# Schedule prices changed, data work taken off GpSimd, and 13 weight pieces of the second MoE converted early and kept in DRAM

## The chip, the cores and the metric

The kernel runs on one core of a Trainium2 chip. Its engines each run their own queue of instructions in order: TensorE (PE, matmuls), VectorE (DVE), ScalarE (ACT), GpSimd (POOL) and SyncE (SP, which here only issues DMAs). The metric is the device time of one execution in microseconds (us), the median of several runs.

## The reference

Three stages follow each other. The weights `w1`, `w2`, `w3`, `w_out` and `w_in` arrive as 64-bit floats, all else as 32-bit.

```python
# attention: 4 batches, 8 heads, 576 tokens, head size 64, mask by blocks of 64
scores = where(block_i >= block_j, scale * q @ k.T, -1e9)
x = softmax(scores) @ v                                  # -> (2304, 512)
# first MoE, d_ff 768
h = maximum(maximum(x @ w1, x @ w2), x @ w3);  y = h @ w_out
# second MoE, d_ff 2048
h = y @ w_in;  g = h * cos(h);  out = g @ w_out          # -> (2304, 512)
```

## The kernel before

**Split products.** Each 32-bit operand is split into a rounded part `hi` and a rest `lo`, and a product is three matmuls (hi·hi, hi·lo, lo·hi). Splitting takes a copy (`R.copy`) and a subtraction (`R.sub`).

**Weights.** `convert` (line 419) makes 32-bit values of a 64-bit piece of 128x512 and splits it: a DMA of 512 KB into `raw`, a scaling of the low words in place (`raw<-raw`) and of the high words (`t<-raw`), three DVE steps on `t` (shift `t<-t`, merge `t<-raw,t`, and the add, which the trace calls CUSTOM_DVE_ANT_0 and the order ISA), the copy to `hi`, the subtraction to `lo`. There are 24 pieces for the first MoE (`whi`/`wlo`, `vhi`/`vlo`) and 32 for the second: 16 of `w_in` and 16 of `w_out`.

**Attention.** There are 32 items, one for a batch, a half of the queries and a pair of heads. An item runs: scores `S` on PE, maxima (`stat<-S`) on DVE, exponentials into `prob` on ACT with sums into `stat`, reciprocal on DVE, scaling of the rows of `prob` (`scale_rows`, line 234, 4 or 5 instructions), transposes `tb`, evacuation to `pt`, product with `v` into `X`, evacuation to `x`, then `xhi` and `xlo`. There is one `prob` buffer, so the next item's exponentials wait for this item's transposes. The first 8 items (`NATIVE`) do not split their operands.

**First MoE as filler.** Whenever 4 items have finished a half of a batch, 22 units of the first MoE (matmuls into `psm` from `xhi`, `xlo`) are queued and PE takes them between attention steps. Their results need the pool `wk`, which opens only once item 7 has used its operands (line 733). Results `y` go to DRAM.

**Second MoE.** The 2304 tokens are five chunks: four of 512 and one of 256. For each of 16 feature pieces `fc` there are 12 matmuls of `hstage` (`psm<-yh`, ...), element work (`th`, `gh`, `gl`), and 12 of `ostage` (`po`). Weight pieces are converted while chunk 0 runs: 7 of `w_in` ahead of it, and in it one of `w_out` for each `fc` and one of `w_in` for every second (lines 849 to 854). Their pool `wc` takes the space of the first MoE's weights and opens when its last matmul is done.

**What sets the order.** All operations are recorded first. `Plan.run` (line 276) then plays them through a list schedule with a price for each (`price`, line 243), emits every engine's instructions in that order, and for those that may run on several engines (`choose`: copies, scalings, subtractions) takes the engine that finishes first by price, with the price multiplied by `WEIGHT` (line 134). So a price moves both the order and the choice of engine. All emitted instructions have line L208 in the trace.

Of the kernel before, what the change touches and what calls it, by code (L numbers as in the profile page):

```python
# [8 lines left out]
F32 = mybir.dt.float32  # L9
F32R = mybir.dt.float32r  # L10
# [4 lines left out]
ALU = mybir.AluOpType  # L15
# [4 lines left out]
P = 128  # L20
# [4 lines left out]
def f32(ap):  # L25
    return ap.bitcast(F32)
# [104 lines left out]
class Plan:  # L131
    CROSS = 35.0
    COLD = 30000.0
    WEIGHT = {"DVE": 2.5, "ACT": 1.0, "POOL": 2.0}

    def __init__(self, tc):
        self.tc, nc = tc, tc.nc
# [105 lines left out]
    def price(self, engine, method, outs, ins, kw):  # L243


        if engine == "SP":
            tiles = outs + ins
            return 600.0, 2000.0 + sum(v.n * v.rows * 4 for v in tiles[:1]) / 240.0, False
        n = outs[0].n
        if engine == "PE":  # L250
            late = 190.0
            if method == "transpose":
                return 109.0, late, False
            dt = ins[0].buf.dt
            if dt == F32:
                return 4 * n / 2.4 + 13, late, False
            load = ins[0].n / 1.2
            return (max(n / 2.4 + 3, 65.0) if dt == BF16 else max(n / 2.4 + 13.5, load)), late, False
        psum = any(v.buf.psum for v in outs + ins)
        if method == "tensor_reduce":  # L260
            n = ins[0].n
        if engine == "ACT":
            scaled = isinstance(kw.get("scale"), View)
            return (n * 0.833 + (55 if psum else 100) + 95 * ("bias" in kw) + 95 * scaled
                    + 93 * ("accum_out" in kw)), 112.0, False
        if engine == "DVE":
            sb = [v for v in ins if not v.buf.psum]
            fast = method in ("tensor_copy", "tensor_scalar", "memset") and not psum
            two = method in ("tensor_tensor", "scalar_tensor_tensor") and len(sb) > 1
            if method == "reciprocal":  # L270
                return 70.0 + 5 * n, 100.0, False
            return n * (0.52 if fast else 1.04) + 68, 88.0, fast or two
        return (n * 2.35 + 75 if method == "tensor_tensor" else n * 1.04 + 90), 45.0, method != "memset"


    def run(self):
# [102 lines left out]
def fused_kernel(tc, qk, v2, w1, w2, w3, wout, w_in2, w_out2, out):  # L379
# [3 lines left out]
    NFF = w1.shape[0]  # L383
    NFC = w_in2.shape[0]
    DM = wout.shape[2]
    NK = DM // P
# [4 lines left out]
    R = Plan(tc)  # L391
    const = R.open(name="const", bufs=1)
    cv = R.open(name="cv", bufs=1)
# [3 lines left out]
    dram = R.open(name="dram", bufs=1, space=DRAM)  # L397
# [48 lines left out]
    for u in range(2):  # L446
        f = Half()
# [130 lines left out]
    def pv(it):  # L578
        f = it.f
        n = f.n  # L580
        h, l = xhi[it.half][:, it.pair], xlo[it.half][:, it.pair]
        where = {}
        for c, (j, b) in enumerate(f.order):
            where.setdefault(j, []).append((c, b))
        if it.native:
            X = ps_x.tile([P, 512], F32, "X", tag="X", bufs=2)
        else:
            x32 = at.tile([P, NLOW], F32, "x32", tag="x32")
        for e in range(2):
            a, o = 64 * e, 64 - 64 * e  # L590
            if not it.native:
                X = ps_x.tile([P, 512], F32, "X", tag="X", bufs=2)
            for j in range(f.nj):
                c0, b0 = where[j][0]
                nb = len(where[j])
                q0 = 64 * (b0 - f.first)
                if not it.native and q0 >= f.both:

                    v = it.vs[:, j, 2 * e:2 * e + 2].rearrange("p a d -> p (a d)")
                    dst = X[:, f.both:2 * n - f.both].then(  # L600
                        lambda ap, q=q0 - f.both: ap.rearrange("p (c q) -> p c q", c=2)[:, :, q:])
                    dst.n = 2 * (n - q0)
                    R.tensor.matmul(dst, v, it.pt[:, :, c0:c0 + nb, a:a + 64], start=j == 0, stop=j == f.nj - 1,
                                    skip_group_check=True)
                    continue
                with R.unit():
                    for i in range(1 if it.native else 2):
                        p = it.pt[:, i, c0:c0 + nb, a:a + 64]
                        if it.native:
                            R.tensor.matmul(X[a:a + 64, q0:n], it.vr[:, j, e], p, start=j == 0,  # L610
                                            stop=j == f.nj - 1, skip_group_check=True)
                        else:
                            v = it.vs[:, j, 2 * e:2 * e + 2].rearrange("p a d -> p (a d)")
                            R.tensor.matmul(X[:, q0:n], v, p, start=j == 0 and i == 0, stop=j == f.nj - 1 and i == 1,
                                            skip_group_check=True)
            if not it.native:
                R.scalar.copy(x32[a:a + 64, :n], X[o:o + 64, :n])
                R.vector.tensor_tensor(x32[a:a + 64, :n], X[a:a + 64, :n], x32[a:a + 64, :n], ALU.add)
                R.vector.tensor_tensor(x32[a:a + 64, f.both:n], X[a:a + 64, n:2 * n - f.both], x32[a:a + 64, f.both:n],
                                       ALU.add)  # L620
        if it.native:
            R.copy(h, X[:, :n])
            R.vector.tensor_tensor(l, X[:, :n], f32(h), ALU.subtract)
        else:
            R.copy(h, x32[:, :n])
            R.sub(l, x32[:, :n], f32(h))
# [49 lines left out]
        return units + [lambda d=d: ygroup(d) for d in range(NK)]  # L676


    def conv_w(n, pool, bufs):
        if n < 3 * NFF:  # L680
            j, m = divmod(n, 3)
            convert((w1, w2, w3)[m][j], whi[j][:, m].rearrange("p k e -> p (k e)"),
                    wlo[j][:, m].rearrange("p k e -> p (k e)"), pool, bufs)
        else:
            j = n - 3 * NFF
            convert(wout[:, j], vhi[:, j], vlo[:, j], pool, bufs)

    NI = len(items)
    LA = 2
    fill, owed, converted = [], [0.0], [0]  # L690
# [3 lines left out]
    def conv_next():  # L694
        n = converted[0]
        if n < 4 * NFF:
            if n % 3 < 2 and not wk:
                conv_w(n, cv_start, 4)
            else:
                conv_w(n, cv, 2)  # L700
            converted[0] += 1

    def units(share):
# [14 lines left out]
    for n in range(NI + 1):  # L718
        conv = CONV.get(n, (0, 0, 0))
        if n:  # L720
            transposes(items[n - 1])
        for step in range(3):
            if step == 1 and n < NI:
                scores(items[n])
                if n + LA < NI:
                    load(items[n + LA])
            if step == 2 and n:
                it = items[n - 1]
                pv(it)
                if it.pair == HP - 1:  # L730
                    if it.n == HP - 1:
                        R.close(cv_start)
                        wk = R.open(cv_start, name="wk", bufs=1)
                    fill += zip([*range(1, 3 * NFF + 1)] + NK * [4 * NFF], moe1_units(it.b, it.half))
            for _ in range(conv[step]):
                conv_next()
            units((0.3, 0.35, 0.35)[step])
        if n + 1 < NI:
            prep(items[n + 1])
    R.close(ps_x)  # L740
    R.close(at)


    chunks = [(t, min(CH, NT - t)) for t in range(0, NT, CH)]
    NA = 7
    wb = R.open(at, name="wb", bufs=1, side="right")
    ps_o = R.open(ps_x, name="ps_o", bufs=1, space=PSUM, side="right")
    ps_h = R.open(ps_x, name="ps_h", bufs=1, space=PSUM, side="right")
# [1 line left out]
    wih, wil, woh, wol = {}, {}, {}, {}  # L750
    raw_from = [0]

    def conv_in(fc, pool):
        raw_from[0] += 1
        wih[fc] = pool.tile([P, NK, P], F32R, f"wih{fc}")
        wil[fc] = pool.tile([P, NK, P], F32R, f"wil{fc}")
        convert(w_in2[fc], wih[fc].rearrange("p k e -> p (k e)"), wil[fc].rearrange("p k e -> p (k e)"),
                (cv, wb)[raw_from[0] % 2], 2)

    def conv_out(fc, pool):  # L760
        raw_from[0] += 1
        woh[fc] = pool.tile([P, DM], F32R, f"woh{fc}")
        wol[fc] = pool.tile([P, DM], F32R, f"wol{fc}")
        convert(w_out2[:, fc], woh[fc], wol[fc], (cv, wb)[raw_from[0] % 2], 2)

    yh, yl = {}, {}

# [37 lines left out]
    def hstage(c, fc):  # L805
        n = chunks[c][1]
        ps = bank()[:, :n]
        prods = [(wih[fc], yh[c]), (wih[fc], yl[c]), (wil[fc], yh[c])]
        for k in range(NK):
            with R.unit():  # L810
                for i, (w, x) in enumerate(prods):
                    R.tensor.matmul(ps, w[:, k], x[:, k, :n], start=(k == 0 and i == 0),
                                    stop=(k == NK - 1 and i == 2))
        t = wk2.tile([P, CH], F32, "th", tag="t", bufs=3)[:, :n]
        gh = wk2.tile([P, CH], F32R, "gh", tag="gh", bufs=3)[:, :n]
# [30 lines left out]
    for n in range(len(seq) + LAG):  # L846
        if n < len(seq):
            c, fc = seq[n]
# [62 lines left out]
```

## Time and profile before

| | us |
|---|---|
| median of 3 runs | 966.83 (965.18 to 967.91) |
| the profiled execution, own time | 967.8 |
| its span, first to last instruction | 966.0 |
| PE busy | 911.8 (94%) |
| DVE busy | 642.9 (67%) |
| ACT busy | 465.4 (48%) |
| POOL busy | 135.4 (14%) |

The profile calls matmul ends modelled, so PE's busy share alone does not say that it runs at its peak; counts of matmuls in a stretch (the x numbers) say more. The program has these stretches: the 8 unsplit items with PE waiting often (to about 94 us), attention with first-MoE filler (to about 520), the last of the first MoE (to about 555), chunk 0 with the weight conversions (to about 645), the other chunks (to the end).

### The profile page before, as it was taken

To read this page: it belongs to the slowest core of one execution; us is meant where nothing else is said; L and a number is where in the kernel's file an instruction comes from. 1 tells how busy PE (TensorE), PEld (TensorE's weight loads), DVE (VectorE), ACT (ScalarE), POOL (GpSimd) and SP (SyncE) were. 2 spreads that over 40 slices of the span, in tenths; PEclk is the share of its full clock that TensorE was granted. 3 is DMA by queue.
4 is the path that set the end of the run, shared out by engine and by line. 5 is a ranking of instruction groups with operands and counts; after the bars stand their busy time and mean duration, and the time that the engine had idled before them with its cause. 6 is when DMAs were issued, how large, how long until landed. Compare 5 with 4: busy or idle time off the path is not lost.

```text
span 966.0 us, 14289 instructions
## 1 busy us (share of the span) xinstructions
PE 911.8 (94%) x5356; PEld 800.2 (83%) x5356; DVE 642.9 (67%) x1286; ACT 465.4 (48%) x1035; POOL 135.4 (14%) x168
## 2 busy tenths in 40 slices
PE   4878999999999999999999999899999999999998
PEld 3645989899998998998999988668888888888897
DVE  5887966677567576576665979996555544555554
ACT  5656455565556565555663566654224222322233
POOL 2322121011111011101011245520000000000000
PEclk9998999999999999999999999999999999999999
DMA  5454441211122111212003534532001000100010
GB/s 166 156 163 153 135 136 50 74 56 36 37 62 63 55 36 43 61 40 85 15 1 105 165 108 148 157 110 88 0 1 50 16 1 1 44 1 1 1 44 23
DMA packets 35749, 64.89 MB, mean 67 GB/s; under 512 B 9312, under 2 KB 20576, under 8 KB 35680
## 3 DMA queue, kind: packets, MB, share of 16 engines
q1 hardware_dynamic: 35680, 63.98, 21.3%
q8 instruction: 42, 0.69, 0.3%
q14 instruction: 27, 0.22, 0.1%
HBM read 54.53 MB, written 9.44 MB: 66 GB/s over the span
## 4 chain that ended last, share of the span: by engine, by line
PE 65%; DVE 17%; ACT 10%; issue 5%; POOL 2%; DMA 1%; ACTq 0%; SPq 0%; DVEq 0%; POOLq 0%
PE psm L208 35%; PE po L208 17%; PE S L208 7%; ACT prob L208 5%; DVE t L208 5%; DVE stat L208 5%; PE tb L208 4%; PE X L208 2%; DVE th L208 1%; DVE hm L208 1%; DVE pt L208 1%; POOL prob L208 1%; ACT hh L208 1%; DVE x L208 1%; DVE vs L208 1%
## 5 line engine op out<-in xcount | busy, mean ns | idle before, releaser
L208 PE MATMUL psm<-xhi,whi 128*128 128x320 f32 (+1 forms) x576 | 176.8, 307 | 4.7 <-DVE hm L208 3.4
L208 PE MATMUL psm<-xlo,whi 128*128 128x320 f32 (+1 forms) x576 | 170.6, 296 | 0.9 <-DVE xlo L208 0.9
L208 PE MATMUL psm<-xhi,wlo 128*128 128x320 f32 (+1 forms) x576 | 170.4, 296 | 0.0
L208 ACT ACTIVATE th<-th,halfpi 128x512 f32<-128x512 f32 (+1 forms) x80 | 54.4, 681 | 162.4 <-DVE th L208 162.4
L208 PE MATMUL psm<-yh,wih 128*128 128x512 f32 (+1 forms) x320 | 119.6, 374 | 5.7 <-ACT wih L208 5.7
L208 DVE TENSOR_REDUCE stat<-S 128x1 f32<-128x320 f32 (+8 forms) x144 | 64.4, 485 | 86.4 <-PE S L208 75.7
L208 PE MATMUL psm<-yh,wil 128*128 128x512 f32 (+1 forms) x320 | 119.6, 374 | 0.7 <-DVE wil L208 0.7
L208 PE MATMUL psm<-yl,wih 128*128 128x512 f32 (+1 forms) x320 | 119.2, 372 | 0.0
L208 PEld LDWEIGHTS psm<-xhi,whi 128*128 128x128 f32 x576 | 109.4, 190 | 6.4 <-DVE hm L208 4.5
L208 PE MATMUL po<-wol,gh 128*128 128x512 f32 x288 | 112.8, 392 | 0.0
L208 PE MATMUL po<-woh,gh 128*128 128x512 f32 x288 | 112.6, 391 | 0.0
L208 PE MATMUL po<-woh,gl 128*128 128x512 f32 x288 | 112.4, 390 | 0.0
L208 POOL TENSOR_SCALAR prob<-prob,stat 128x64 f32<-128x64 f32 (+8 forms) x100 | 63.2, 647 | 351.1 <-DVE stat L208 273.0
L208 PEld LDWEIGHTS psm<-xlo,whi 128*128 128x128 f32 x576 | 109.4, 190 | 1.2 <-DVE xlo L208 1.1
L208 PEld LDWEIGHTS psm<-xhi,wlo 128*128 128x128 f32 x576 | 109.1, 189 | 0.0
L208 ACT ACTIVATE prob<-S,stat 128x128 f32<-128x128 f32 (+8 forms) x144 | 74.7, 528 | 62.6 <-DVE stat L208 62.1
L208 DVE TENSOR_SCALAR th<-psm 128x512 int32<-128x512 f32 (+1 forms) x80 | 50.7, 635 | 57.7 <-PE psm L208 52.1
L208 DVE TENSOR_TENSOR th<-psm,th 128x512 f32<-128x512 f32 (+1 forms) x80 | 50.9, 636 | 51.0 <-ACT th L208 51.0
L208 PE MATMUL tb<-ident,prob 128*128 128x128 f32 x400 | 64.9, 286 | 13.9 <-DVE pt L208 6.6
L208 PEld LDWEIGHTS psm<-yh,wih 128*128 128x128 f32 x320 | 60.6, 189 | 17.9 <-ACT wih L208 6.6
L208 DVE TENSOR_TENSOR gl<-th,gh 128x512 fp32r<-128x512 f32 (+1 forms) x72 | 46.6, 647 | 42.4 <-ACT gh L208 42.2
L208 PEld LDWEIGHTS psm<-yh,wil 128*128 128x128 f32 x320 | 60.6, 189 | 12.9 <-DVE wil L208 1.9
(99 smaller groups left out, 1805.9 us busy)
## 6 DMA issues: line engine op xcount, KB each, us to landing
raw<-w SPq DMA_DIRECT2D x18, 512.0 KB, 3.8
raw<-w_in SPq DMA_DIRECT2D x16, 512.0 KB, 3.4
raw<-w_out SPq DMA_DIRECT2D x16, 512.0 KB, 3.7
vr<-v SPq DMA_DIRECT2D x16, 320.0 KB, 3.2
qk<-qk SPq DMA_DIRECT2D x12, 416.0 KB, 3.2
out<-osb SPq DMA_DIRECT2D x18, 256.0 KB, 2.0
qk<-qk SPq DMA_DIRECT2D x12, 320.0 KB, 3.0
vr<-v SPq DMA_DIRECT2D x16, 192.0 KB, 2.5
```

What stands on the lines that cost most here:

```text
L208: return lambda: getattr(real, method)(*[value(a) for a in args], **{k: value(a) for k, a in kw.items()})
```

## The change

Three things change. (1) `WEIGHT` of POOL goes from 2 to 100, so the schedule never chooses POOL: its 159 data instructions move to DVE and ACT (DVE goes from 1288 to 1419 instructions, ACT from 893 to 921, PE stays at 5250). (2) Prices change: POOL's, outputs with gaps (+120 ns on ACT and DVE), and the two additions that read `X` across partitions (+118 ns). (3) While items after number 9 run, `ahead()` converts 13 pieces of the second MoE (9 of `w_in`, 4 of `w_out`) into a buffer `both` and stores it to DRAM as `kept`; chunk 0 loads these with one DMA each. The remaining 19 pieces are converted as before. `hi` and `lo` of a piece now share one tile, which the order names `w_in` or `w_out`.

```diff
-    WEIGHT = {"DVE": 2.5, "ACT": 1.0, "POOL": 2.0}
+    WEIGHT = {"DVE": 2.5, "ACT": 1.0, "POOL": 100.0}
...
+        spread = 120.0 * (outs[0].hi - outs[0].lo + 1 > n)
...
-        return (n * 2.35 + 75 if method == "tensor_tensor" else n * 1.04 + 90), 45.0, method != "memset"
+        return (n * 3.3 + 75 if method == "tensor_tensor" else max(400.0, n * 1.04 + 195)), 45.0, method != "memset"
...
-                R.vector.tensor_tensor(x32[a:a + 64, :n], X[a:a + 64, :n], x32[a:a + 64, :n], ALU.add)
+                R.vector.tensor_tensor(x32[a:a + 64, :n], X[a:a + 64, :n], x32[a:a + 64, :n], ALU.add).cost += 118.0
...
+    NA = 7
+    AHEAD = [("in", fc) for fc in range(NA, NFC)] + [("out", fc) for fc in range(3, NFC - 1, 3)]
+    kept = {}
+
+    def ahead():
+        if len(kept) < len(AHEAD) and converted[0] == 4 * NFF:
+            kind, fc = AHEAD[len(kept)]
+            both = cv.tile([P, 2, 512], F32R, "both", tag="raw", bufs=CVR)
+            convert(w_in2[fc] if kind == "in" else w_out2[:, fc], both[:, 0], both[:, 1], cv, CVR)
+            kept[kind, fc] = dram.tile([P, 2, 512], F32, f"kept_{kind}{fc}")
+            R.sync.dma_start(kept[kind, fc], f32(both))
...
+        if n > 9 and n % 3:
+            ahead()
...
+    def conv(kind, fc, pool, src):
+        w = pool.tile([P, 2, 512], F32R, f"w_{kind}{fc}")
+        if (kind, fc) in kept:
+            R.sync.dma_start(f32(w), kept[kind, fc])
+        else:
+            raw_from[0] += 1
+            convert(src, w[:, 0], w[:, 1], (cv, wb)[raw_from[0] % 2], 2)
+        return w
```

The scaling of the first item of the second half of batch 0 (item 4) stands like this on POOL before:

```order
L208 TENSOR_SCALAR prob<-prob,stat_162 128x384
L208 TENSOR_SCALAR prob<-prob,stat_162 128x448
L208 TENSOR_SCALAR prob<-prob,stat_162 128x512
L208 TENSOR_SCALAR prob<-prob,stat_162 128x576
L208 TENSOR_SCALAR prob<-prob,stat_253 128x384
```

and like this on DVE now, where the reciprocal is followed by two of the four at once:

```order
L208 TENSOR_SCALAR stat_169<-stat_169 128x4
L208 ISA t<-raw,t 128x1024
L208 RECIPROCAL stat_169<-stat_169 128x4
L208 TENSOR_SCALAR prob<-prob,stat_169 128x512
L208 TENSOR_SCALAR prob<-prob,stat_169 128x576
L208 TENSOR_TENSOR wlo_466<-t,whi_445 128x512
```

The other two (384 and 448) stand on ACT now. POOL has no row of `prob` left.

In the attention stage, DVE around the first split item's output (`x`, then `xlo`) reads before:

```order
L208 TENSOR_TENSOR x_1498<-X,x_1498 64x320
L208 TENSOR_TENSOR vs<-vr,vs 128x3x128
L208 TENSOR_TENSOR x_1498<-X,x_1498 64x192
L208 TENSOR_TENSOR x_1498<-X,x_1498 64x320
L208 TENSOR_TENSOR x_1498<-X,x_1498 64x192
L208 CAST xhi_234<-x_1498 128x320
L208 TENSOR_TENSOR pt<-tb,pt 128x512
L208 TENSOR_TENSOR xlo_239<-x_1498,xhi_234 128x320
```

and now, with one early conversion (`t`, then `both`) and the start of the next behind `xlo`:

```order
L208 TENSOR_TENSOR x_1356<-X,x_1356 64x192 x2
L208 TENSOR_SCALAR t<-t 128x512
L208 TENSOR_TENSOR xlo_248<-x_1356,xhi_245 128x320
L208 SCALAR_TENSOR_TENSOR t<-raw,t 128x512
L208 ISA t<-raw,t 128x1024
L208 TENSOR_TENSOR both<-t,both 128x512
L208 TENSOR_TENSOR hm<-psm,hm 128x256 x2
L208 TENSOR_TENSOR hl<-hm,hh 128x256
L208 TENSOR_TENSOR hm<-psm,hm 128x256
L208 TENSOR_SCALAR t<-t 128x512
```

The evacuations of the filler (`hm`) now have conversion steps ahead of them.

On SP, at the end of the first MoE (its last stores are `y_1_...`), the queue before alternates loads of both weights:

```order
L208 DMA y_1_6209<-hm 128x256 x2
L208 DMA raw<-w_in 128x1024
L208 DMA y_1_6209<-hm 128x256 x2
L208 DMA raw<-w_out 128x1024 x2
L208 DMA raw<-w_in 128x1024
L208 DMA raw<-w_out 128x1024 x2
L208 DMA raw<-w_in 128x1024
```

and now it loads `w_out` and then all 13 kept pieces in a row, of which the first rows are:

```order
L208 DMA raw<-w_out 128x1024 x2
L208 DMA y_1_6308<-hm 128x256
L208 DMA raw<-w_out 128x1024
L208 DMA w_in_6436<-kept_in_1452 128x1024
L208 DMA w_in_6443<-kept_in_1565 128x1024
L208 DMA w_out_6451<-kept_out_3178 128x1024
L208 DMA w_in_6460<-kept_in_1830 128x1024
```

After chunk 0's first `th` DVE had 21 of the ISA steps before, and has 8 now.

## Rows read from the trace of the kernel before

**Rows 1.** Windows: busy us (count) by engine, clock, DMA share, GB/s.
```profile
0.00:94.00 94.00, 66.68 (x306) 44.09 (x307) 68.97 (x175) 55.56 (x137) 24.86 (x41) 0.93 0.51 157
130.00:260.00 130.00, 124.00 (x895) 117.63 (x895) 86.70 (x197) 72.95 (x190) 18.82 (x28) 1.00 0.21 63
260.00:388.00 128.00, 122.75 (x887) 117.23 (x887) 85.22 (x194) 72.75 (x190) 17.57 (x29) 1.00 0.18 52
388.00:516.00 128.00, 122.69 (x885) 117.36 (x884) 83.77 (x192) 71.95 (x188) 15.48 (x27) 1.00 0.13 40
516.00:560.00 44.00, 44.00 (x338) 42.78 (x337) 34.14 (x64) 22.58 (x44) 8.34 (x10) 1.00 0.53 175
560.00:600.00 40.00, 40.00 (x176) 32.62 (x175) 38.31 (x59) 26.79 (x45) 19.25 (x15) 1.00 0.33 100
600.00:650.00 50.00, 43.57 (x179) 33.94 (x178) 47.49 (x73) 29.66 (x51) 24.31 (x12) 0.97 0.44 137
650.00:700.00 50.00, 50.00 (x220) 40.91 (x218) 29.67 (x45) 17.73 (x29) 0.00 (x0) 1.00 0.15 48
```

**Rows 2.** Waits of PE between 590 and 660 us: total, times, longest.
```profile
PE psm L208 <- ACT wih L208: 5.7, 2, 4.2
```

**Rows 3.** Chain that ended last, 0 to 105 us: start, us, what.
```profile
41.52 2.49 POOL prob L208 x5
...
66.55 0.14 POOL prob L208
66.69 0.93 issue
67.62 2.19 POOL prob L208 x3
...
93.73 7.24 PE psm L208 x48
```

**Rows 4.** Waits of PE weight loads, 100 to 530 us.
```profile
PEld tb L208 <- DVE pt L208: 11.1, 21, 1.1
```

**Rows 5.** Groups by form on DVE, 560 to 650 us: busy us, mean ns.
```profile
L208 DVE CUSTOM_DVE_ANT_0 t<-raw,t 128x1024 uint16<-128x1024 uint16 x21 | 17.5, 848 | 0.0
L208 DVE SCALAR_TENSOR_TENSOR t<-raw,t 128x512 int32<-128x512 int32 x21 | 17.3, 838 | 0.0
L208 DVE TENSOR_SCALAR t<-t 128x512 int32<-128x512 int32 x21 | 12.2, 593 | 0.4 <-ACT t L208 0.4
L208 DVE TENSOR_TENSOR gl<-th,gh 128x512 fp32r<-128x512 f32 x6 | 5.2, 869 | 0.6 <-ACT gh L208 0.6
```

**Rows 6.** The same view, 130 to 516 us.
```profile
L208 DVE TENSOR_TENSOR hl<-hm,hh 128x320 fp32r<-128x320 f32 x16 | 7.9, 492 | 6.4 <-ACT hh L208 6.3
...
L208 DVE CUSTOM_DVE_ANT_0 t<-raw,t 128x1024 uint16<-128x1024 uint16 x2 | 1.4, 692 | 0.1
L208 DVE SCALAR_TENSOR_TENSOR t<-raw,t 128x512 int32<-128x512 int32 x2 | 1.4, 680 | 0.0
...
L208 DVE TENSOR_TENSOR vlo<-t,vhi 128x512 fp32r<-128x512 f32 x1 | 0.7, 695 | 0.0
...
L208 DVE TENSOR_SCALAR prob<-prob,stat 128x576 f32<-128x576 f32 x1 | 0.5, 512 | 0.0
...
L208 DVE TENSOR_SCALAR t<-t 128x512 int32<-128x512 int32 x1 | 0.4, 414 | 0.0
```

**Rows 7.** Groups by form on POOL, 560 to 650 us.
```profile
L208 POOL TENSOR_TENSOR wol<-t,woh 128x512 fp32r<-128x512 f32 x9 | 16.3, 1828 | 19.6 <-ACT woh L208 19.6
L208 POOL TENSOR_TENSOR gl<-th,gh 128x512 fp32r<-128x512 f32 x8 | 14.6, 1834 | 20.4 <-issue 14.5 <-ACT gh L208 5.7
```

**Rows 8.** DMA issues: KB each, median us from issue to landing.
```profile
raw<-w_in SPq DMA_DIRECT2D x16, 512.0 KB, 3.4
```

**Rows 9.** Chain that ended last, 530 to 660 us.
```profile
558.86 1.75 DMA y<-hm
```

**Rows 10.** Groups by form on ACT, whole span.
```profile
L208 ACT ACTIVATE prob<-prob,stat 128x384 f32<-128x384 f32 x11 | 6.8, 617 | 0.8 <-DVE stat L208 0.6
```

More of the change, by code (lines that the diff above doesn't have):

```diff
@@ L261, in price @@
             n = ins[0].n
+        spread = 120.0 * (outs[0].hi - outs[0].lo + 1 > n)
         if engine == "ACT":
             scaled = isinstance(kw.get("scale"), View)
-            return (n * 0.833 + (55 if psum else 100) + 95 * ("bias" in kw) + 95 * scaled
+            return (n * 0.833 + spread + (55 if psum else 100) + 95 * ("bias" in kw) + 95 * scaled
                     + 93 * ("accum_out" in kw)), 112.0, False
@@ L271, in price @@
                 return 70.0 + 5 * n, 100.0, False
-            return n * (0.52 if fast else 1.04) + 68, 88.0, fast or two
-        return (n * 2.35 + 75 if method == "tensor_tensor" else n * 1.04 + 90), 45.0, method != "memset"
+            return n * (0.52 if fast else 1.04) + 68 + spread, 88.0, fast or two
+        return (n * 3.3 + 75 if method == "tensor_tensor" else max(400.0, n * 1.04 + 195)), 45.0, method != "memset"
     def run(self):
@@ L617, in pv @@
                 R.scalar.copy(x32[a:a + 64, :n], X[o:o + 64, :n])
-                R.vector.tensor_tensor(x32[a:a + 64, :n], X[a:a + 64, :n], x32[a:a + 64, :n], ALU.add)
+                R.vector.tensor_tensor(x32[a:a + 64, :n], X[a:a + 64, :n], x32[a:a + 64, :n], ALU.add).cost += 118.0
                 R.vector.tensor_tensor(x32[a:a + 64, f.both:n], X[a:a + 64, n:2 * n - f.both], x32[a:a + 64, f.both:n],
-                                       ALU.add)
+                                       ALU.add).cost += 118.0
         if it.native:
@@ L676, in moe1_units @@
         return units + [lambda d=d: ygroup(d) for d in range(NK)]
+    CVR = 2
     def conv_w(n, pool, bufs):
@@ L699, in conv_next @@
             else:
-                conv_w(n, cv, 2)
+                conv_w(n, cv, CVR)
             converted[0] += 1
@@ L744, in fused_kernel @@
     chunks = [(t, min(CH, NT - t)) for t in range(0, NT, CH)]
-    NA = 7
     wb = R.open(at, name="wb", bufs=1, side="right")
@@ L751, in fused_kernel @@
     raw_from = [0]
-    def conv_in(fc, pool):
[L754 to L758, printed above, removed]
+    def conv(kind, fc, pool, src):
[6 more added lines that the diff above has]
+        return w
+    def conv_in(fc, pool):
+        w = conv("in", fc, pool, w_in2[fc])
+        wih[fc], wil[fc] = ([w[:, i, k * P:(k + 1) * P] for k in range(NK)] for i in range(2))
     def conv_out(fc, pool):
[L761 to L764, printed above, removed]
+        w = conv("out", fc, pool, w_out2[:, fc])
+        woh[fc], wol[fc] = w[:, 0], w[:, 1]
     yh, yl = {}, {}
@@ L811, in hstage @@
                 for i, (w, x) in enumerate(prods):
-                    R.tensor.matmul(ps, w[:, k], x[:, k, :n], start=(k == 0 and i == 0),
+                    R.tensor.matmul(ps, w[k], x[:, k, :n], start=(k == 0 and i == 0),
                                     stop=(k == NK - 1 and i == 2))
```

## The prediction

> **What bounds the kernel now.** I read the table by stretches first [rows 1], because the share of PE over the whole span (94%) hides three different states; then the waits of PE where the conversions run [rows 2], the chain in the first stretch [rows 3], and the waits of PE's weight loads in attention [rows 4].
>
> In the dense part, 650 to 700 us, PE issues 220 matmuls in 50 us, one each 0.227 us [rows 1]. That is the yardstick for chunk 0: 560 to 600 us has 176, and 176 x 0.227 = 40.0 us, so PE is full there although DVE is busy 38.3 of 40. From 600 to 650 us there are 179, so 41 are missing, 41 x 0.227 = 9.3 us. DVE is busy 47.5 of 50 there and the largest wait of PE is for a converted piece (`wih`), 5.7 us in 2 times [rows 2]. So conversions bound only these 50 us, and all that moving them can give back is about 9 us.
>
> Two more places hold idle PE. In the first 94 us PE is busy 66.7, idle 27.3; DVE is busy 69.0 and ACT 55.6 of the 94, so no engine is full: the chain steps from engine to engine, with POOL's scaling of `prob` as a link, until the filler starts at 93.7 us [rows 3]. From 130 to 516 us PE is idle 6.0 + 5.3 + 5.3 = 16.6 of 386 us, with DVE busy 255.7 (66%) [rows 1]; the largest wait there is that of transposes for `pt`, 11.1 us in 21 times, 0.53 us each [rows 4]. Elsewhere PE is full. Its number of matmuls does not change, so the change can act only through these idle times: 27 at the start, 17 in attention, 9 in chunk 0.
>
> **Chunk 0, fewer conversions.** DVE is busy 38.3 + 47.5 = 85.8 us of the 90 from 560 to 650 [rows 1]. Its conversions there fall from 21 to 8. One costs 0.848 + 0.838 + 0.593 = 2.28 us in this stretch [rows 5]; successive DVE instructions overlap by about 0.08 us each (my estimate: the durations of rows 5 and 6 against the busy time), so 13 of them take away about 28 us. Beside GpSimd the same three steps cost 2.28, where POOL is seldom busy 0.692 + 0.680 + 0.414 = 1.79 [rows 6]: 0.49 x 8 = 4 us less on the remaining 8. Against that DVE takes back what POOL did: 8 `gl` and 3 `yl` at 0.695, which is what the subtraction of that size costs without POOL's company [rows 6], 8 us. The 9 `wol` and 3 `wil` of POOL belong to pieces of which 13 have gone, so they add nothing net. DVE comes to 85.8 - 28 - 4 + 8 = about 62 of 90 us. From 516 to 560 us DVE is at 78% and PE has no idle time [rows 1], so PE becomes the bound and the 9.3 us come back; I take 9, with 5 as the lower end for waits that show up where DVE is late by an order the schedule did not foresee.
>
> The Trainium skill speaks against taking work off GpSimd here: its page "Perfetto Trace Analysis", section "Optimizing Scalar/DVE Operations", says that with DVE saturated, offloading even to GpSimd may make sense, and adds that the two share a read port, so that it might not help. By its first half alone, POOL's 23 subtractions of this stretch at 0.695 would put DVE at 101.8 of 90 us and cost 12 us. The trace goes with its second half: POOL needs 1.83 us for what DVE does in 0.695 [rows 6, 7], and DVE's own steps are longer beside it. With 13 conversions gone the first half has no hold.
>
> **The kept pieces.** The loads replace conversions with one DMA of 512 KB. A load of this size lands in 3.4 us [rows 8]; 13 in a row on SP, if none overlapped, take 44 us. They stand behind the last `y` stores, and those land at about 560.6 us [rows 9], so the last piece is there by 605. The first is wanted by the H step of `fc` 7, some 144 matmuls after PE begins chunk 0 at about 555 us: 555 + 144 x 0.227 = 588; the last at the 16th H step, past 625. So the loads lie beside matmuls with 20 us to spare; without that cover the price would be up to 3.4 us a piece. The stores during attention cost one SP entry each. Behind a store that waits for its subtraction stand loads of `qk` and `vr`; these run two items ahead, and 8 items take 130 us, so 16 us an item cover the wait. I cost both at 0.
>
> **The first 94 us, scaling without POOL.** The four POOL scalings of an item of the second half take 0.14 + 0.93 + 2.19 = 3.3 us of the chain; the five of one of the first half 2.5 [rows 3]. Now they are shared. ACT needs 0.62 for 384 columns [rows 10], DVE 0.51 for 576 [rows 6]. Of the seven items whose scaling lies before 93.7 us, two have two on each engine (about 1.3 us, gain 2.0 each), one has all four on ACT (about 2.5, gain 0.8), and four of the first half are mixed or all on DVE (about 1.2, gain 1.3 each): 4.0 + 0.8 + 5.2 = 10 us. Against it DVE gets 16 more scalings of 0.25 to 0.51 us (some 6 us) and two subtractions (1.4), so it rises from 69 to about 74 us of what would be 84 to 90, and part of these stand ahead of a maximum or a reciprocal that the chain waits for. I take 6, nearest the middle, because I cannot tell from the order which of them do. Ends: 11 gained (all of it, and the conversions a little shorter), 3 lost (all of DVE's 7 us on the chain and only 4 of the 10 gained).
>
> **Attention, more work on DVE.** From 130 to 516 us DVE gets: 13 conversions at 0.414 + 0.680 + 0.692 + 0.695 = 2.48 us [rows 6], 32 us; some 48 scalings at about 0.39 us, 19; 17 subtractions that POOL did at about 0.47, 8; together 59, so 255.7 + 59 = 315 of 386 us (82%). Eight of the conversions fall in the first of the three stretches: 86.7 + 8 x 2.48 + 8.5 = 115 of 130, 88%. Cover: PE has filler queued, and lost nothing at 78% (516 to 560 us) or at 96% (560 to 600 us) [rows 1]. For a gain speaks that POOL's steps, which were late against their prices, are gone, and that the additions of `X` and the outputs with gaps are now priced nearer to their times. I take 0, ends 6 gained and 10 lost.
>
> **The sum.** 9 + 6 + 0 = 15 us. The profiled execution took 967.8 us (span 966.0 plus 1.8), so 952.8; the median of the runs lies 1.0 lower, so 952.
>
> **Rivals.**
> - Only chunk 0 gains: the start stays at 94 us since DVE's extra steps take what POOL's scaling gave. For it: DVE is at 73% there already; against it: 3.3 us of an item were on POOL alone. 966.8 - 9 = 958.
> - All three gain by their upper ends: 11 + 6 + 9 = 26, so 941. For it: contention with POOL ends everywhere; against it: DVE at 88%.
> - The kept loads arrive late, or PE waits for something else in chunk 0, and the start gives nothing: the time stays at 966 to 967. Against it: the 20 us of cover.
> - DVE becomes the bound in attention and the kernel is slower. Place: items 9 to 23, where the conversions stand ahead of `hm` and `pt`. Price: 16 items with four groups of transposes, each waiting 0.53 us as the 21 do now [rows 4], are 34 us, against about 11 us idle there now: 23 lost, less the 15: 975. It decides from about 1 us more of PE wait for each of the 16 items. For it: 88% in the first stretch, where PE runs in a fixed order; against it: 96% in 560 to 600 us, where PE lost nothing.
>
> **How the numbers follow.** The forecast (945 to 955) 0.45; only chunk 0 (955 to 963) 0.22; all gain (937 to 945) 0.15; no change 0.06; slower by DVE 0.12. A measurement here tells 0.3% (2.9 us) from no change. Faster by more than that: 0.45 + 0.15 and nearly all of 0.22, 0.80; within it 0.06 and the rest, 0.08; slower 0.12. The range leaves out the slower rival and the lower part of the best case: 941 to 966; the likeliest case alone has 945 to 955.
>
> **What would show it.** Chunk 0: some 220 matmuls in every 50 us from the end of the first MoE, no wait of PE for a weight, DVE near 70%; a wait for a kept load would prove the third rival. Start: the filler's long run of `psm` begins at about 88 us and not at 94; at 94 or later the first rival holds. Attention: idle PE near 17 us; transposes waiting for `pt`, or filler waiting for `hm`, by 30 us or more would be the last rival. DVE's steps of a conversion at 1.8 us in all stretches would show that the longer ones were due to POOL; if they stay at 2.28, that part is wrong.

## The result, and the profile after

| | median us (lowest to highest) | profiled execution | its span |
|---|---|---|---|
| before | 966.00 (964.74 to 967.91) | 967.80 | 966.0 |
| changed | 955.46 (955.11 to 955.84) | 955.45 | 953.7 |

The ratio is 0.9882, 95% interval 0.9868 to 0.9895: 10.5 us less by the medians, 12.3 us by the two profiled spans. The forecast was 952.

The stretches of the changed kernel, in the columns of [rows 1] and in the same stretches but the last:

```profile
0.00:94.00 94.00, 70.06 (x343) 50.51 (x344) 74.12 (x204) 62.35 (x157) 1.88 (x9) 0.91 0.52 163
130.00:260.00 130.00, 124.57 (x899) 119.02 (x900) 106.52 (x245) 85.54 (x209) 0.00 (x0) 1.00 0.35 117
260.00:388.00 128.00, 123.39 (x887) 117.43 (x886) 105.17 (x247) 85.09 (x210) 0.00 (x0) 1.00 0.33 106
388.00:516.00 128.00, 122.83 (x885) 117.53 (x884) 86.14 (x203) 75.26 (x195) 0.00 (x0) 1.00 0.13 41
516.00:560.00 44.00, 44.00 (x332) 42.38 (x331) 37.57 (x79) 24.26 (x48) 0.00 (x0) 1.00 0.62 201
560.00:600.00 40.00, 40.00 (x175) 32.31 (x174) 35.88 (x64) 18.67 (x30) 0.00 (x0) 1.00 0.61 218
600.00:650.00 50.00, 50.00 (x217) 40.53 (x216) 35.34 (x59) 19.14 (x31) 0.00 (x0) 1.00 0.22 64
```

Where 179 matmuls went from 600 to 650 us there are now 217, PE without idle time. The whole list of PE's waits between 530 and 660 us, against the 5.7 us of [rows 2] alone, is one line (total, times, longest):

```profile
PEld psm L208 <- DVE th L208: 0.3, 1, 0.3
```

No wait for a weight is left, neither for a converted piece nor for a kept one. The chain that ended last, cut at 130 us, shows when the filler's long run begins (start, us, what; in [rows 3] it was 93.73):

```profile
85.18 0.70 ACT prob L208 x3
85.88 1.91 issue
87.78 0.43 ACT hm L208
88.21 0.04 issue
88.26 28.43 PE psm L208 x192
```

And the largest wait of the weight loads from 100 to 530 us, 11.1 us in 21 times in [rows 4]:

```profile
PEld tb L208 <- DVE pt L208: 11.6, 23, 1.5
```

**Stages.** For the comparisons I cut each profiled execution at four matmuls of its timeline: the 25th of the filler that reads `x` (start of the long run), the 432nd of these, the first of `hstage`, and the 192nd of `hstage`. The stages are the start, attention 1, attention 2 (with the last of the first MoE), and chunk 0; what follows them takes 320.0 to 322.3 us in every kernel here. "Idle" is PE's idle time from 90 to 550 us, and "clock" what a lowered granted clock took there: the missing share of full clock times the length, summed over slices of 10 us. In e4 and e8 that part lies wholly in the start, which ends later there. The stages come from one execution each: that of e3 lies 3.6 us above the median of its kernel, e1 3.1, e13 2.8, e6 2.0 and the kernel before 1.8 above, e2 2.3 below, the others within 1.3. So stage times of the named ones can be off by that much.

| kernel | median us | ratio to before (95%) | start | att. 1 | att. 2 | chunk 0 | idle | clock |
|---|---|---|---|---|---|---|---|---|
| before | 966.00 | | 93.7 | 87.4 | 373.6 | 89.0 | 16.8 | 0.0 |
| changed | 955.46 | .9868 to .9895 | 88.3 | 90.1 | 373.0 | 80.4 | 16.7 | 0.0 |
| e1_no_early | 962.56 | .9948 to .9970 | 88.8 | 91.3 | 372.3 | 91.5 | 17.2 | 1.7 |
| e2_early_only | 969.39 | 1.0008 to 1.0036 | 92.6 | 88.5 | 381.2 | 81.3 | 21.9 | 0.0 |
| e3_old_prices | 969.56 | 1.0018 to 1.0043 | 88.2 | 92.3 | 385.1 | 83.9 | 26.5 | 5.1 |
| e4_pool_allowed | 963.17 | .9953 to .9979 | 99.2 | 88.0 | 371.5 | 81.0 | 15.5 | 3.0 |
| e8_start_scale_pool | 968.24 | 1.0004 to 1.0023 | 104.8 | 88.2 | 372.0 | 80.6 | 19.3 | 3.4 |
| e9_no_spread | 965.64 | .9978 to .9997 | 85.8 | 96.4 | 378.7 | 81.8 | 23.2 | 5.2 |
| e10_no_118 | 957.35 | .9886 to .9919 | 87.0 | 91.9 | 373.4 | 80.3 | 20.0 | 0.0 |
| e6_add_price | 960.64 | .9918 to .9950 | 87.6 | 92.8 | 377.7 | 80.8 | 19.3 | 3.4 |
| e11_gaps_act_only | 963.19 | .9943 to .9973 | 87.9 | 90.6 | 380.4 | 80.3 | 22.9 | 0.0 |
| e12_gaps_not_raw | 958.30 | .9892 to .9922 | 86.1 | 95.5 | 371.3 | 81.6 | 17.2 | 3.4 |
| e13_cross_70 | 965.79 | .9976 to 1.0005 | 91.1 | 95.7 | 375.2 | 82.9 | 20.3 | 5.1 |
| e5_early_late | 955.06 | .9855 to .9888 | 88.7 | 90.2 | 372.9 | 80.2 | 16.6 | 0.0 |

The 12.3 us of the spans are 5.4 (start) - 2.7 (attention 1) + 0.6 (attention 2) + 8.6 (chunk 0) + 0.4 (the rest).

### The profile page after: what moved, and what is told of

Its sections match the earlier page's. It is cut to its first block, busy times and chain, and to the rows that moved or that the text cites. A ratio compares the mean times of both kernels' runs of the same rounds, so it can differ in the third digit from the quotient of the medians.

```text
span 953.7 us, 14211 instructions
## 1 busy us (share of the span) xinstructions
PE 909.4 (95%) x5356; PEld 801.0 (84%) x5356; DVE 666.7 (70%) x1417; ACT 475.6 (50%) x1063; POOL 1.9 (0%) x9
## 4 chain that ended last, share of the span: by engine, by line
PE 68%; DVE 13%; ACT 7%; issue 2%; ACTq 0%; DVEq 0%
PE psm L208 39%; PE po L208 21%; ACT prob L208 5%; PE S L208 5%; DVE stat L208 4%; PE tb L208 2%; DVE x L208 2%; DVE pt L208 1%; PE X L208 1%; DVE qbd L208 1%; DVE hm L208 1%; DVE vs L208 1%; DVE t L208 1%; DVE prob L208 1%; ACT qbd L208 1%
## 5 line engine op out<-in xcount | busy, mean ns | idle before, releaser
L208 PE MATMUL psm<-yh,w_in 128*128 128x512 f32 (+1 forms) x640 | 195.6, 371 | 0.0
L208 PE MATMUL po<-w_out,gh 128*128 128x512 f32 x576 | 178.7, 391 | 0.0
L208 PEld LDWEIGHTS psm<-yh,w_in 128*128 128x128 f32 x640 | 117.1, 188 | 22.7 <-DVE th L208 0.3
L208 PEld LDWEIGHTS po<-w_out,gh 128*128 128x128 f32 x576 | 106.9, 188 | 23.2 <-ACT gh L208 0.4
L208 PE MATMUL psm<-yl,w_in 128*128 128x512 f32 (+1 forms) x320 | 118.7, 371 | 0.0
L208 PE MATMUL po<-w_out,gl 128*128 128x512 f32 x288 | 112.4, 390 | 0.0
L208 DVE TENSOR_TENSOR gl<-th,gh 128x512 fp32r<-128x512 f32 (+1 forms) x80 | 51.1, 638 | 44.9 <-ACT gh L208 44.4
L208 ACT CAST gh<-th 128x512 fp32r<-128x512 f32 (+1 forms) x76 | 44.0, 578 | 56.4 <-DVE th L208 56.4
L208 PEld LDWEIGHTS psm<-yl,w_in 128*128 128x128 f32 x320 | 60.2, 188 | 11.6
L208 PEld LDWEIGHTS po<-w_out,gl 128*128 128x128 f32 x288 | 54.1, 188 | 11.8 <-DVE gl L208 0.2
## 6 DMA issues: line engine op xcount, KB each, us to landing
w_in<-kept_in SPq DMA_DIRECT2D x9, 512.0 KB, 10.3
```

The costliest lines, as they stand in the source:

```text
L208: return lambda: getattr(real, method)(*[value(a) for a in args], **{k: value(a) for k, a in kw.items()})
```

## The experiments

All edits are made to the changed kernel.

### Which part does what

**e1_no_early**: no piece is converted early.

```diff
-    AHEAD = [("in", fc) for fc in range(NA, NFC)] + [("out", fc) for fc in range(3, NFC - 1, 3)]
+    AHEAD = []
```

> The change without the 13 early pieces: GpSimd gets no data, the prices are new, all 32 pieces are converted as before. Theory (start and chunk 0 are separate gains): the filler's long run begins at 88 us as in the changed kernel; in chunk 0 DVE has 85.8 - 10 (no lengthening beside GpSimd) + 16 (23 subtractions back at 0.695) = 92 of 90 us, so PE loses 9 to 12 us there; 955.5 + 9 to 12 = 964 to 967. Rival (freeing DVE of GpSimd is what counts in chunk 0, the early pieces are beside the point): chunk 0 is dense without them, 955 to 958.

Chunk 0 takes 91.5 us, and DVE is full there again although GpSimd does nothing (windows of this kernel):

```profile
560.00:600.00 40.00, 39.10 (x170) 31.51 (x169) 38.45 (x69) 27.92 (x46) 0.00 (x0) 1.00 0.36 112
600.00:650.00 50.00, 46.30 (x183) 35.47 (x182) 47.25 (x85) 29.84 (x50) 0.00 (x0) 0.93 0.43 127
```

PE issues 183 matmuls in the second stretch and not 217. So it is the early pieces that make chunk 0 dense; freeing DVE of GpSimd's company does not. By the medians they are worth 962.56 - 955.46 = 7.1 us, a little less than the 9 to 12 expected. (This profiled run took 965.68, 3.1 above its median, so its 11.1 us of chunk 0 are too many.) The start is as in the changed kernel, and so is the loss in attention 1: neither comes from the early pieces.

**e2_early_only** and **e3_old_prices**: e3 takes the three price changes back, e2 also lets the schedule use POOL again, so that only the early pieces are left of the change.

```diff
+    WEIGHT = {"DVE": 2.5, "ACT": 1.0, "POOL": 2.0}        # e2 alone
...
+        spread = 0.0                                      # both
...
+        return (n * 2.35 + 75 if method == "tensor_tensor" else n * 1.04 + 90), 45.0, method != "memset"
...
+    ALU.add).cost += 0.0                                  # both additions of X
```

> The 13 early pieces alone: GpSimd allowed as before, old prices. Theory: the long run begins at 93 to 94 us as before, chunk 0 is dense (8.6 us back), 966.0 - 8.6 = 957 to 958. Rival (without GpSimd's removal DVE is still late in chunk 0 or in attention): 962 to 966.

> The changed kernel with the old prices (GpSimd still gets nothing, the pieces are early). Theory (the prices move little): 955 to 957. Rival (orders by measured prices save PE's waits in attention): 959 to 962, with more PE waits between 130 and 516 us.

Both are slower than either expectation. They keep most of the gain in chunk 0 (81.3 and 83.9) and are nevertheless slower than before: attention 2 takes 381.2 and 385.1 us where the changed kernel takes 373.0. From 130 to 516 us, e3 and then the changed kernel:

```profile
130.00:516.00 386.00, 361.28 (x2571) 345.11 (x2570) 291.30 (x678) 239.65 (x605) 0.00 (x0) 0.99 0.27 87
```

```profile
130.00:516.00 386.00, 370.79 (x2667) 353.98 (x2668) 297.83 (x694) 245.89 (x612) 0.00 (x0) 1.00 0.27 88
```

DVE is no busier in e3 (291.3 against 297.8 us), yet PE idles 24.7 us against 15.2. Its wait for `pt` is two thirds longer than the changed kernel's 11.6:

```profile
PEld tb L208 <- DVE pt L208: 19.3, 20, 2.6
```

The longest of these waits, on PE's weight loads and then on DVE (start, us, what; the number in brackets is the idle time before it):

```profile
319.84 0.14 PEld L208 LDWEIGHTS tb<-ident,prob 128*128 128x128 f32 x1 [2.56 <-DVE pt L208]
319.85 0.25 PEld L208 LDWEIGHTS psm<-hh,vhi 128*128 128x128 f32 x1
```

```profile
316.89 0.87 DVE L208 TENSOR_TENSOR x<-X,x 64x192 f32<-64x192 f32 x2
317.79 0.42 DVE L208 TENSOR_TENSOR hm<-psm,hm 128x256 f32<-128x256 f32 x1
318.25 0.36 DVE L208 TENSOR_TENSOR x<-X,x 64x192 f32<-64x192 f32 x1
318.64 0.43 DVE L208 TENSOR_SCALAR t<-t 128x512 int32<-128x512 int32 x1
319.10 0.69 DVE L208 TENSOR_TENSOR pt<-tb,pt 128x512 fp32r<-128x512 f32 x1
```

Filler (`psm<-hh,vhi`) stands ready behind the transpose and cannot pass it. A step of an early conversion (`t<-t`, 0.43 us) does stand ahead of `pt`, as the slower rival had it, but more of the wait goes to additions of `x` and to `hm`. And e2 loses 8 us in attention 2 without a longer wait for `pt`:

```profile
PEld tb L208 <- DVE pt L208: 10.6, 21, 1.1
```

Its list has 5.6 us for POOL's `prob` instead, which the changed kernel has not. So what keeps the loss off is what the prices decide and not DVE's spare share. The prices decide two things that no run here separates: the order, and the engine of some steps (between e3 and the changed kernel, 36 of DVE's instructions stand on ACT and 24 the other way).

The start of e3 (88.2) also shows that its gain needs no price: POOL's removal gives it, and e2, with POOL, has 92.6.

**e4_pool_allowed** (weight 2 for POOL, its new price) and **e8_start_scale_pool** (POOL scales `prob` in the first 8 items and does nothing else):

```diff
-    WEIGHT = {"DVE": 2.5, "ACT": 1.0, "POOL": 100.0}
+    WEIGHT = {"DVE": 2.5, "ACT": 1.0, "POOL": 2.0}        # e4
```

```diff
-            R.scale_rows(p, p, st[:, 5 + i:6 + i])
+            if it.native:                                 # e8
+                R.gpsimd.tensor_scalar(p, p, st[:, 5 + i:6 + i], 1.0, ALU.mult, ALU.mult)
+            else:
+                R.scale_rows(p, p, st[:, 5 + i:6 + i])
```

> The changed kernel with GpSimd allowed again at its new prices (weight 2); the pieces are early. Theory: scaling on GpSimd stands in the chain of the start again, long run at 92 to 94 us, chunk 0 dense, 957 to 959. Rival (the correct price of GpSimd is enough, its removal is not needed): 953 to 955.5.

> The changed kernel, but the scaling of prob in the 8 unsplit items (36 instructions) is put on GpSimd again, at GpSimd's new price. Theory (that link is what the start gained): the filler's long run begins at 92 to 95 us instead of 88, chunk 0 stays dense, 958 to 961. Rival (the start gained from another thing, such as shorter conversion steps on DVE): long run at 88 to 89 us, 955 to 956.

Both are slower than either expectation. Chunk 0 and attention 2 are within 1.5 us of the changed kernel; the difference is in the start, 10.9 and 16.5 us longer. That is well beyond the kernel before, which also scaled on POOL (93.7). The granted clock has a part in it: its mean over the start is 0.86 and 0.85, and 0.90 in the changed kernel, which is 13.9, 15.7 and 8.8 us of missing clock; PE does not bound the start throughout, so the 5 and 7 us between them are upper bounds. Weight loads of e8 up to 108 us:

```profile
PEld tb L208 <- ACT pt L208: 9.3, 8, 3.4
PEld X L208 <- ACT pt L208: 8.8, 4, 7.4
PEld S L208 <- ACT prob L208: 6.8, 6, 2.8
PEld tb L208 <- POOL prob L208: 6.4, 11, 1.0
```

The wait for POOL is 6.4 us; more than that is added by a single wait of 7.4 us for an evacuation on ACT that the new order puts late. So these two show that POOL in the start costs, not that it costs 11 or 16 us: the order of ACT changed with it, and I did not separate the two. The clean pair is e2 and e3, which differ in POOL's weight alone: 92.6 against 88.2. The direct row is in the trace of before, up to 108 us, where the largest wait for another engine's work was

```profile
PEld tb L208 <- POOL prob L208: 8.7, 14, 1.7
```

It is gone from the changed kernel. In its place the wait of `S` for `stat` on DVE grew from 1.1 to 3.7 us. The start's gain is not the clock's: the mean clock of the start was 0.93 before (6.6 us missing) and is 0.90 now.

### Which price, and why it helps

**e9_no_spread**: outputs with gaps get no surcharge. **e10_no_118**: the additions that read `X` get none.

```diff
-        spread = 120.0 * (outs[0].hi - outs[0].lo + 1 > n)
+        spread = 0.0                                      # e9
...
-                R.vector.tensor_tensor(x32[a:a + 64, :n], X[a:a + 64, :n], x32[a:a + 64, :n], ALU.add).cost += 118.0
+                R.vector.tensor_tensor(x32[a:a + 64, :n], X[a:a + 64, :n], x32[a:a + 64, :n], ALU.add).cost += 0.0    # e10, both
```

> The changed kernel without the price for outputs with gaps (+120 ns). With old prices throughout, attention took 12 us longer than in the changed kernel. Theory A (this price is what matters, through the choice of engine and the order of qbd and vs): most of 12 us, 963 to 968, attention (from the end of the first 432 products of the first MoE to the first H step) 380 to 385 us instead of 373. Theory B (the additions of X matter): 955 to 957.

> The changed kernel without the 118 ns on the two additions of X. Theory B (this price matters, because the additions stand at the end of each item's chain and DVE is 82% busy): 962 to 968, attention 380 to 385 us instead of 373. Theory A (outputs with gaps matter): 955 to 957. If each gives a part, both runs lie between 957 and 963.

Without the surcharge on gaps all but 1 us of the change's gain is gone: 6.3 us more in attention 1, 5.7 in attention 2, with 2.5 less in the start, where its clock is higher (0.98 against 0.90). Against the changed kernel 75 instructions stand on the other one of DVE and ACT. The 118 ns are worth about 2 us.

Is the surcharge good because it is true? By the starts on the changed kernel's timeline (lower quartile), on ACT the gap is there: `qbd` of 320 columns is followed by the next start after 491 ns (old price 366), `vs` of 384 after 536 (420). On DVE `vs` of 384 takes 466 ns (old price 467); for `qbd` the starts leave it open (399 ns at the tenth percentile, 504 at the quartile, old price 400). So **e11_gaps_act_only** keeps it on ACT alone, and **e6_add_price** sets another surcharge, that of a conversion's add (275 ns in both kernels), to zero; the trace has 600 ns from its start to the next, which is its price without it.

```diff
-            return n * (0.52 if fast else 1.04) + 68 + spread, 88.0, fast or two
+            return n * (0.52 if fast else 1.04) + 68, 88.0, fast or two            # e11
...
-        R.vector.tensor_tensor(i32(t), i32(t), low, ALU.add).cost += 275.0
+        R.vector.tensor_tensor(i32(t), i32(t), low, ALU.add).cost += 0.0           # e6
```

> The changed kernel with the price for outputs with gaps on ACT alone. The traces show that ACT's copies with gaps take some 115 to 125 ns more between starts than the old price (qbd of 320: 491 ns against 366; vs of 384: 536 against 420) and DVE's none (vs of 384: 466 against 467). If true prices are what helps: 954 to 957, no stage longer than in the changed kernel by over 2 us. If spare time in the plan is what helps: attention longer by 2 to 5 us, 957 to 961.

> The changed kernel with the conversion's add priced at 600 ns as it runs (successive starts 600 ns apart) instead of 875. If what counts is that prices equal the measured times: 952 to 955. If what counts is spare time in the plan, which the 275 ns give it on every conversion: slower, 957 to 963, with more waits of PE between 130 and 390 us.

Both tables, the second clearly truer than the one of the changed kernel and the first so for `vs`, give slower kernels: 963.19 (beyond both its expectations) and 960.64, attention 2 at 380.4 and 377.7. The prices do not help by being right.

Then perhaps as spare time for late steps? The time of e6 fits that expectation (957 to 963). **e13_cross_70** gives such time everywhere, by doubling the plan's delay for a hand-over between instructions. **e12_gaps_not_raw** takes the surcharge from the scaling of `raw` alone.

```diff
-    CROSS = 35.0
+    CROSS = 70.0                                          # e13
...
+        spread = 120.0 * (outs[0].hi - outs[0].lo + 1 > n and outs[0].buf.dt != I32)    # e12
```

> The changed kernel with every hand-over between instructions planned 35 ns longer (70 instead of 35). If spare time in the plan helps: fewer waits of PE in attention, attention 368 to 371 us instead of 373, 950 to 954. If only prices of particular steps count: 955 to 960.

> The changed kernel with the price for outputs with gaps on qbd and vs, not on the scaling of raw in the conversions (whose true excess on ACT is some 40 ns). If that price helps through the conversions alone: as without the price at all, the stretch from the long run's begin to product 432 of the first MoE 96 us instead of 90, in all 961 to 966. If through qbd and vs: that stretch 90, attention 373, 954 to 957. If each has its stage: first stretch 96, attention 373, 959 to 962.

More spare time everywhere is no better: 965.79, slower than either expectation, with 5.6 us lost in attention 1, 2.2 in attention 2, 2.8 in the start and 2.5 in chunk 0. e12 (958.30, near the expectation that each has its stage) shows places: the surcharge on `raw` is worth 5.4 us in attention 1 (95.5 without it), less 2.2 that the start loses by it, and nothing in attention 2, where the one on `qbd` and `vs` is at work. Most of the 5.4 us lie at one wait in attention 1, for a `w_out` piece of the first MoE:

```profile
PEld psm L208 <- ACT vhi L208: 3.8, 3, 3.3
```

Behind its longest, of 3.3 us, the granted clock is at 0.50 from 135.5 to 142.3 us, 3.4 us of clock. So the surcharge acts at particular steps, by the order or the choice of engine that it happens to give.

**e5_early_late**: the early pieces are recorded in items 18 and on, and not in two of every three from 10 on.

```diff
-        if n > 9 and n % 3:
+        if n > 17:
```

> The changed kernel with the early pieces spread over items 18 to 30 instead of 10 to 28, behind the first batch's filler. If the early pieces load DVE in the first half of attention enough to matter: 1 to 3 us faster, 952 to 954.5. If DVE's load at 82% is covered anyway: the same, 955 to 956.

955.06, the same as the changed kernel within the scatter of both, with every stage within 0.4 us. But the edit did not move the pieces: the schedule gives every engine the same instructions in the same order as in the changed kernel, and the 13 subtractions into `both` start at 145 to 339 us there and at 146 to 340 here. So this run is the changed kernel measured again, and whether it matters where the pieces lie in attention is not tested. No version here is clearly faster than the changed kernel.

### What an unlucky order costs

The sum of the two attention stages follows the last two columns of the table, but for e4 and e8, whose start reaches into them. From the changed kernel to e3 idle time and clock grow by 9.8 + 5.1 = 14.9 us and the stages by 14.3; to e9 by 6.5 + 5.2 = 11.7 and 12.0; to e11 by 6.2 + 0 and 7.9. How the clock comes in is seen in slices of 1 us of e9_no_spread (the number before the last two is the granted clock):

```profile
133.00:134.00 1.00, 0.87 (x6) 0.60 (x5) 1.00 (x3) 1.00 (x4) 0.00 (x0) 1.00 0.00 0
134.00:135.00 1.00, 0.00 (x0) 0.00 (x0) 1.00 (x5) 0.94 (x3) 0.00 (x0) 1.00 0.00 0
135.00:136.00 1.00, 0.00 (x0) 0.00 (x0) 1.00 (x4) 0.00 (x0) 0.00 (x0) 1.00 0.27 49
136.00:137.00 1.00, 0.38 (x2) 0.22 (x2) 0.97 (x5) 0.78 (x3) 0.00 (x0) 1.00 1.01 336
137.00:138.00 1.00, 0.98 (x3) 0.42 (x3) 1.00 (x3) 1.00 (x3) 0.00 (x0) 0.64 0.78 307
138.00:139.00 1.00, 0.50 (x3) 0.36 (x3) 0.94 (x3) 1.00 (x4) 0.00 (x0) 0.50 0.09 37
...
143.00:144.00 1.00, 1.00 (x6) 1.00 (x5) 0.54 (x2) 0.37 (x2) 0.00 (x0) 0.50 0.22 78
144.00:145.00 1.00, 1.00 (x8) 1.00 (x7) 0.00 (x0) 1.00 (x4) 0.00 (x0) 0.95 0.00 0
145.00:146.00 1.00, 1.00 (x9) 1.00 (x8) 0.68 (x2) 0.25 (x1) 0.00 (x0) 1.00 0.00 0
```

PE stands still from 134 to 136 us and does little to 137; then the clock is at 0.50, the lower of its two levels (1.2 GHz), until 144, with 6 matmuls in a microsecond and not 9. The wait behind it, 128 to 142 us:

```profile
PEld tb L208 <- ACT prob L208: 4.4, 5, 3.0
```

A single wait of 3.0 us, and 3.5 us of clock on top (0.14 x 10 in the slice from 130, 0.21 x 10 in the next). The length of one wait does not decide it alone: e1 and e6 have a fall of the clock right behind waits of 1.7 and 1.8 us, while e10 and e11, with longest waits of 1.9 and 2.0 us, have none from 90 to 550 us. Nor does a loss need the clock: e2 and e11 lose 6.6 and 7.9 us in attention with the clock column at 0.0. In the changed kernel the longest wait of the weight loads from 100 to 530 us is 1.5 us, and its clock is at 1.00 in every slice of 10 us from 90 to 550.

## Why the prediction was right or wrong, by its steps

**Chunk 0: right.** 9 us forecast, 8.6 in the spans and 7.1 in the medians of e1's pair. Of the 9.3 us of missing matmuls, 6.4 were idle PE (50 - 43.57) and 1.5 the clock that fell behind the 4.2 us wait (0.97 of 50 us) [rows 1, 2]; both are gone. DVE did not come down to 62 of 90 us but to 35.88 + 35.34 = 71.2. The conversions are as forecast in number and price:

```profile
L208 DVE CUSTOM_DVE_ANT_0 t<-raw,t 128x1024 uint16<-128x1024 uint16 x8 | 5.5, 686 | 0.1
L208 DVE SCALAR_TENSOR_TENSOR t<-raw,t 128x512 int32<-128x512 int32 x8 | 5.5, 685 | 0.0
L208 DVE TENSOR_SCALAR t<-t 128x512 int32<-128x512 int32 x8 | 3.3, 422 | 0.0
L208 DVE TENSOR_TENSOR gl<-th,gh 128x512 fp32r<-128x512 f32 x18 | 12.4, 689 | 4.0 <-ACT gh L208 3.7
L208 DVE TENSOR_TENSOR yl<-t,yh 128x512 fp32r<-128x512 f32 x8 | 5.4, 687 | 0.0
```

Three steps make 0.686 + 0.685 + 0.422 = 1.79 us, the forecast figure, against 2.28 beside GpSimd [rows 5]. What the sum left out is that a denser PE brings more element work into the same 90 us (18 `gl` where DVE and POOL had 14, and 53 `th` steps where there were 47) and that 8 `yl` fall to DVE, not the 4 it had counted (one on DVE, three on POOL). A small slip goes the same way: 13 conversions of 2.28 us less 39 overlaps of 0.08 are 26.5 us, not 28. With 79% PE still lost nothing, so the time did not depend on it.

The Trainium skill, page "Perfetto Trace Analysis", section "Optimizing Scalar/DVE Operations", had been weighed here: with DVE saturated, offloading even to GpSimd may make sense. Where DVE stays full, no price for it is shown: chunk 0 takes 91.5 us without GpSimd in e1 and 89.0 with it before, but 2.5 us are less than the 3.1 by which e1's execution lies above its median, and far from the 12 that the prediction reckoned. Where 13 conversions have gone there is none either: 81.0 with GpSimd (e4), 80.4 without.

**Kept pieces at no cost: right.** They landed later than the 3.4 us of [rows 8], at a median of 10.3 and 9.5 us (the 16 DMA engines were at least 90% busy from 552 to 576 us), and PE waited for none:

```profile
w_in<-kept_in SPq DMA_DIRECT2D x9, 512.0 KB, 10.3
w_out<-kept_out SPq DMA_DIRECT2D x4, 512.0 KB, 9.5
```

**The start: the size right, the end wrong.** 6 us forecast, 5.4 measured, long run at 88 as said. DVE is busy 68.4 of the start's 88.3 us and not 74 (the 74.1 up to 94 us take in the first filler), so its added work was over-counted. But the prediction took the start as time won for good, and 2.7 us of it are lost again in attention 1 (87.4 to 90.1) for the same 626 matmuls. PE's idle time there rises from 3.0 to 4.2 us; the other 1.5 are in time in which PE counts as busy, and no view here tells why. From 88 to 180 us the changed kernel has waits of PE for weights that the trace of before does not show there:

```profile
PEld psm L208 <- DVE vlo L208: 1.2, 2, 0.6
PEld psm L208 <- DVE vhi L208: 1.0, 1, 1.0
```

These are `w_out` pieces of the first MoE, which DVE converts along with what POOL did. But e2 has such waits too (1.3 and 1.1 us) and takes 88.5, so they are not enough to explain it. All kernels with POOL at work in the start have 87.4 to 88.5 there, all without it 90.1 to 96.4. The former also start the filler later, so whether POOL's work on DVE or the earlier start is the reason stays open. This term, which the prediction did not have, is most of the 3.5 us between 952 and 955.46; another 1.0 is the step from the profiled execution to the median, which the changed kernel does not show (955.45 and 955.46).

**Attention at nothing: the right number for a wrong reason.** Attention 2 came out at 373.0 after 373.6, and that is luck as far as the prediction's reason goes. The cover named was the queued filler, with DVE at 82%; DVE is at 297.8 of 386 us, 77%, lower than forecast. e2 and e3 have the same cover, the same pieces and no higher a share of DVE (73% and 75%), and lose 8 and 12 us. The failed step is the argument from the share: PE runs in a fixed order, and filler that is queued behind a transpose covers nothing while that transpose waits for `pt`. The prediction gave DVE as the bound in attention 0.12, priced at 23 us lost. Its mechanism, steps of DVE ahead of `pt`, is seen in e3; the price was too high, and the condition another: what the prices decide, not the load. The prices were named as a possible gain here and are what the term hangs on: without the gap surcharge the two attention stages lose 12 us, and the kernel all but 1 us of its gain.

**The rivals.** "Only chunk 0 gains" (958) lies near the time but not by its mechanism: the start did gain. "All gain by their upper ends" fails on attention. "Kept loads late" fails on the list of waits.

**What stays open.** Why one plan of nearly equal instructions waits 1.5 us at worst and another 3.0 us was followed to the waits named above, not to the plan's decision that makes them. None of the experiments gave a rule for setting such prices, and none separates the order from the choice of engine.

## What to carry to other kernels

In a list schedule with fixed queues, the sum of busy times does not tell whether added work is covered: look at PE's idle time and at its granted clock in the stretch, and then at the waits behind them. One wait of 3.0 us was followed here by 3.5 us of lowered clock. A price table is a knob on the order and on the choice of engine, and not only a model of time: test each price alone, and a truer one can be slower (two of two here). After an edit to what is recorded, compare the emitted orders first: the one of e5 changed nothing. Parts of a change are not additive either: here the early pieces alone lose 0.2%, the rest of it without them gains 0.4%, and both together gain 1.2%.

## What was not expected of the hardware

- DVE's steps are longer only beside GpSimd: the three of a conversion take 2.28 us in chunk 0 before and 1.79 with GpSimd idle, in all 56 conversions of the changed kernel (add: mean 687 ns). The kernel before shows it by itself: its 39 adds beside which no GpSimd instruction runs take 676 to 694 ns, the 17 others 653 to 1816.
- After PE had stood still for 2.8 to 3.0 us, the granted clock fell from 1.00 to 0.50 and stayed there while PE was busy again (137 to 144 us in e9, 135.5 to 142.3 in e12); the single waits of up to 1.5 us in the changed kernel's attention brought no fall. Between the two the runs differ, as said above.
- Where early pieces are loaded in one stretch, the core's DMA moved 293 GB/s over 40 us (e3, 560 to 600 us) and 218 in the changed kernel, with no wait of PE for them in either.
